# Attention, an MLP and a top-2 mixture of experts in one kernel: ranking queued later, five early groups, first softmax scaled on ScalarE, two 128-row groups last

## The chip, the cores and the metric

The kernel runs on one core of a Trainium2 chip. The metric is the device time of one execution in microseconds (us). The engines are TensorE (PE, with its weight loads as PEld), VectorE (DVE), ScalarE (ACT), GpSimd (POOL) and SyncE (SP, which here issues most transfers). Each takes its instructions in the order in which the program wrote them, so an instruction that waits holds up all behind it on its engine.

## What is computed

Three stages, each feeding the next, for T = 2304 tokens of 512 numbers, all in float32 accuracy:

```python
scores = scale * q @ k.T                       # 4 batches, 8 heads, 576 positions, 64 per head
scores = where(0 <= i - j < 128, scores - slope[h] * abs(i - j), -1e9)
attn = exp(scores - max);  attn /= attn.sum() + 1e-9
x = (attn @ v) as (2304, 512)
x = softplus(x @ w_in) @ w_out                 # 512 -> 2048 -> 512
noisy = x @ w_gate + log1p(exp(x @ w_noise)) * noise      # 8 experts
top2, weights = the two largest of each token, softmax over the two
out[token] += weight * (relu(x[token] @ w1[e]) @ w2[e])   # 512 -> 1024 -> 512, for each choice e
```

## The kernel before

**Tiles.** The MLP works on nine chunks of 256 tokens and on sixteen slices of its 2048 hidden columns. A step t is one slice of one chunk: `mm1` (12 products of 128x256 columns, rows `h<-xh,w` and `h<-xl,w`), a softplus that passes through ACT, DVE and POOL, and three steps later `mm2` (rows `y<-w,gh` and `y<-w,gl`). Numbers are split in a high and a low part (`xh`, `xl`; `gh`, `gl`; `whi`, `wlo`), so one product takes three passes.

**Order of the work.** The first six slices of every chunk run first, and the attention units (20 blocks of up to 128 query rows, four steps m of two heads each) are fed in between, as each chunk's input needs them. Then the last ten slices of chunk 0, of chunk 1 and so on to chunk 8. After each of these a chunk's result is complete, and its routing is fed in by `route(c)`: one entry per half step, where `None` is a half step with nothing. The routing steps are the transposes of the result, the gate's product (`r_logits`), its transposition back (`r_sum`, rows `t<-ident,lgp`) with a chain of some twenty small DVE instructions that finds the two experts (`r_top2`, which ends in the marks `r_mb`), and the ranking `r_rank` (rows `t<-r_mb,tri`): small products that count how many tokens chose each expert so far. The rank is the token's place in its expert's list, and four scatters per chunk write the token and its weight there (`rect<-rec,pi`, issued from POOL; each waits until the one before has landed).

**Groups.** The experts' stage works on groups of one expert: pairs of 128 rows (256 rows, high and low parts) and singles (128 rows, in plain float32). Which expert and which rows a group has is only known at run time. A small table on DVE holds it: `early_table` after the count of chunk 6, for groups that are already full, and `late_table` after chunk 8, for the others. SP reads the table into registers, loads each group's list (`rc<-rect`) and its weights (eight tiles of 512 KB, `raw2` or `rawp`), and POOL gathers the rows (`xg<-x1buf,rc`), 128 at a time. PE transposes them (`t<-ident,xg`). A pair has eight rounds, each an up product (`h<-xh,whi` and the like) and a down product. At the end of a group each 128 rows are scaled (`ys`) and added to the output by a scatter that accumulates (`out<-ys,rc`); such scatters also wait for each other.

**Planner.** The order on each engine is set by the class `Order`: the program is written in PE's order, and it keeps a rough clock with an assumed cost for each instruction. A `chain` is a list of instructions on other engines; each is written out when the clock says that it could run. What is written by the planner runs in that order, whatever the real durations are. In a chain, "A" is ACT, "V" DVE, "P" POOL.

**The lines that the change touches.** In `step_a`, a pair of head blocks gets its scores by PE, DVE adds the bias and finds the maximum, ACT takes the exponential and its sum, DVE the reciprocal (`rec`, lines 357 and 358), and `norm` (line 362) multiplies both blocks by it on POOL; only then can PE transpose them (`step_b`). In `w_convert` the first weights of the MLP (stored as float64) are made from their two integer halves by ACT, DVE and POOL; its last instruction `low` (line 495) runs on DVE or, for each third tile, on POOL. The main loop calls `early_table` at `last_start`, the first step of chunk 8's last ten. The constants `NEARLY` and `nsure` fix how many groups of which kind there are.

Of the kernel before, what the change touches and what calls it, by code (L numbers as in the profile page):

```python
# [99 lines left out]
def cv(n):  # L100
    return 0.15 + n * 0.00104
# [6 lines left out]
def cg(n):  # L108
    return 0.05 + n * 0.00275
# [3 lines left out]
def moe_chain_kernel(ctx, tc, qk, v, w_in, w_out, w_gate, w_noise, noise, w1, w2, out):  # L113
# [18 lines left out]
    NCV = 5  # L132
    NPAIR = (2 * T // P + E - 1) // 2 - 3
    NSING = E - 1
    NEARLY = 3
    NOPT = 2
    NLATE = NPAIR - NEARLY
    TPAD = T + P
# [185 lines left out]
    def step_a(m0):  # L324
# [7 lines left out]
        for x in range(2):  # L332
            hp = (m0 + x) % 4
            for j in range(2):
# [2 lines left out]
                          qkT[hd, sl, 1, hp, :], start=True, stop=True)  # L337
                spend(2.0 * n / 2.4)
        st = tl(att, [P, 4, 4], F32, "st", NST, ("a", m0 + 1))
        for x in range(2):  # L340
            s = tl(att, [P, 512], F32, "s", NS, ("be", m0 + x))
            s = s.rearrange("p (h t) -> p h t", h=2)
            M[m0 + x] = dict(s=s)
            for j in range(2):
                def tail(s=s, x=x, j=j):
                    DVE.tensor_tensor_reduce(s[:nq, j, :n], ps[j][:nq, x, :n],
                                             relh[:nq, 2 * (m0 % 4 + x) + j, r0:r0 + n],
                                             -(D ** -0.5), 3.0e38, OP.add, OP.min, st[:nq, 0, 2 * x + j:2 * x + j + 1])

                def ex(s=s, x=x, j=j):  # L350
                    y = slice(2 * x + j, 2 * x + j + 1)
                    ACT.activation(s[:nq, j, :n], s[:nq, j, :n], AF.Exp, bias=st[:nq, 0, y], scale=-1.0,
                                   accum_out=st[:nq, 1, y])
                chain(("V", cv(n), tail, ("ttr", m0 + x, j)), ("A", ca(n) + 0.2, ex, ("ex", m0 + x, j)))
# [4 lines left out]

        def norm(x):  # L360
            s = M[m0 + x]["s"]
            POOL.tensor_tensor(s[:nq, :, :n], s[:nq, :, :n],  # L362
                               st[:nq, 3, 2 * x:2 * x + 2, None].to_broadcast([nq, 2, n]), OP.mult)
        chain(("V", 0.6, rec, None, [("ex", m0 + x, j) for x in range(2) for j in range(2)]),
              ("P", cg(2 * n), lambda: norm(0), ("a", m0)), ("P", cg(2 * n), lambda: norm(1), ("a", m0 + 1)),
              after=4 * cv(n) + ca(n) + 0.4)

    def step_b(m):
# [98 lines left out]
    def w_convert(i):  # L467
# [24 lines left out]

        def low():
            t = W[i]
            (DVE if LOWV[i % len(LOWV)] else POOL).tensor_tensor(t[:, 1], f32(d["a"]), f32(t[:, 0]), OP.subtract)

        def store():
            if i in sidx:
# [3 lines left out]
              ("A", ca(512), first), ("A", ca(512), third), ("V", 2.2, bits),  # L502
              ("P", cg(512), lambda: POOL.tensor_tensor(d["a"], d["a"], d["raw"][:, :, 0], OP.add), ("wa", i)),
              ("A", ca(512), high),
              ("V", cv(512), low, ("wl", i)) if LOWV[i % len(LOWV)] else ("P", cg(512), low, ("wl", i)),
              (None, 0.0, lambda: mark_now(("w", i), ("wl", i))),
              ("SP", 0.06, store, ("st", i)))

# [259 lines left out]
    def route(c):  # L768
        for _ in range(3):
            yield None  # L770
        yield lambda: r_transpose(c, 0)
        yield lambda: r_transpose(c, 1)
        if c + 1 < NCH:
            yield lambda: part_load(c + 1)
        yield lambda: r_logits(c)
        yield None
        yield lambda: r_sum(c)
        yield None
        yield None
        yield None  # L780
        yield lambda: r_rank(c)
        if c == NCH - 1:
            yield None
            yield lambda: late_table(c)
# [216 lines left out]
    ip = is_ = 0  # L1001
    nsure = NSING - NOPT
    while ip < NLATE or is_ < nsure:
        if ip == NLATE or (is_ + 1 < nsure and is_ * NLATE <= (ip - 2) * nsure):
            groups.append((1, "singles", is_))
            is_ += 1
        else:
            groups.append((2, "pairs", ip))
            ip += 1
# [304 lines left out]
    for t in range(NT + max(L2, len(items) + 2)):  # L1314
# [18 lines left out]
            fed, gap, gaps = 0, 0, 2 * n - 2  # L1333
        if t == last_start:
            open_p2()
            early_table(NCH - 3)
        if t < NT:
            c, fc = jobs[t]
# [91 lines left out]
```

## Time and profile before

| | us |
|---|---|
| median of three runs (1182.83 to 1188.4) | 1184.91 |
| the profiled execution | 1184.44 |
| its span, first to last instruction | 1182.6 |
| PE busy | 1085.8 (92%) |
| DVE busy | 733.9 (62%) |
| ACT busy | 615.2 (52%) |
| POOL busy | 529.3 (45%) |

TensorE's clock is granted at one of two levels, 1.2 and 2.4 GHz. The profile gives it as a share of the full one; the mean is 0.960 here. PE's idle time and the stretches at the lower level are spread unevenly: the page's slices show PE below nine tenths in the first three, in the 22nd, in the 25th and in the last of forty. The shares of a whole run say little about what one stage waits for, so the stages are read apart.

### The profile page before, as it was taken

Reading aid. Unit: us, or ns where it says so; the run is one execution under the profiler, and the core shown is the slowest. Engines: PE = TensorE matmul, PEld = TensorE weight load, DVE = VectorE, ACT = ScalarE, POOL = GpSimd, SP = SyncE. Lnnn points to the kernel's source line nnn. Section 1 sums busy time; section 2 is a strip of 40 time slices with the busy share of each in tenths; the row PEclk is TensorE's granted clock in tenths of the full one; section 3 lists DMA queues with packets and bytes.
Section 4 is the critical chain, followed back from the end, with each engine's and each line's share of the span. In section 5 each row is a group of like instructions: output and inputs, shape, how many; then the busy total and the mean of one; then the engine's idle time right before and its main releaser. Section 6 shows DMA issues by size and latency. Waiting matters only on the chain. (4 is left out here: it accounts for less than half of the span.)

```text
span 1182.6 us, 20591 instructions
## 1 busy us (share of the span) xinstructions
PE 1085.8 (92%) x7021; PEld 924.0 (78%) x7021; DVE 733.9 (62%) x1896; ACT 615.2 (52%) x1443; POOL 529.3 (45%) x547
## 2 busy tenths in 40 slices
PE   4689999999999999999996994999999999999995
PEld 3467777777788888888875894988988988989993
DVE  8985798988875565565567683544544545635640
ACT  5676787877754444444434451544544545535531
POOL 3765677866665555556555131123223222223211
PEclk8689999999999999999997997999999999999998
DMA  7231443555673211212209429779789788788722
GB/s 293 98 90 54 174 167 129 206 196 179 215 271 117 74 70 55 72 46 64 72 23 391 121 53 352 215 211 292 213 241 263 210 248 262 207 259 251 190 36 28
DMA packets 79276, 198.31 MB, mean 168 GB/s; under 512 B 17153, under 2 KB 27521, under 8 KB 79169
## 3 DMA queue, kind: packets, MB, share of 16 engines
q1 hardware_dynamic: 68832, 175.43, 44.2%
q0 software_dynamic: 10336, 21.54, 9.3%
q8 instruction: 56, 0.92, 0.3%
q14 instruction: 52, 0.42, 0.1%
HBM read 157.70 MB, written 39.25 MB: 167 GB/s over the span
## 5 line engine op out<-in xcount | busy, mean ns | idle before, releaser
L190 PE MATMUL h<-xh,w 128*128 128x256 f32 x1152 | 243.7, 294 | 5.0 <-ACT xh L420 2.6
L1235 POOL DMA_INDIRECT out<-ys,rc x41 | 82.4, 2010 | 350.4 <-DVE ys L1244 207.9
L190 PEld LDWEIGHTS h<-xh,w 128*128 128x128 f32 x1152 | 194.3, 196 | 18.5 <-DVE sl L559 6.4
L1121 DVE TENSOR_TENSOR wlo<-rawp,whi 128x1024 fp32r<-128x1024 f32 x106 | 129.5, 1222 | 117.5 <-ACT whi L1123 117.3
L190 PE MATMUL y<-w,gh 128*128 128x512 f32 x552 | 182.8, 413 | 1.0 <-DVE x L633 1.0
L190 PE MATMUL h<-xl,w 128*128 128x256 f32 x576 | 166.4, 289 | 4.1 <-DVE xl L425 4.1
L1123 ACT ACTIVATE whi<-rawp 128x1024 fp32r<-128x1024 f32 x106 | 112.3, 1059 | 110.0 <-PE h L190 102.5
L190 PE MATMUL h<-xh,whi 128*128 128x256 f32 x576 | 165.8, 288 | 0.0
L565 POOL TENSOR_TENSOR su<-sa,su 128x256 f32<-128x256 f32 x144 | 111.0, 771 | 119.4 <-DVE su L564 83.8
L190 PE MATMUL h<-xh,wlo 128*128 128x256 f32 x576 | 163.0, 283 | 0.0
L190 PE MATMUL h<-xl,whi 128*128 128x256 f32 x576 | 163.0, 283 | 0.0
L556 ACT ACTIVATE sa<-h 128x256 f32<-128x256 f32 x144 | 54.9, 381 | 169.0 <-PE h L190 133.6
L560 POOL TENSOR_TENSOR sl<-sl,su 128x256 f32<-128x256 f32 x144 | 110.8, 770 | 22.0 <-DVE sl L559 13.4
L190 PEld LDWEIGHTS h<-xl,w 128*128 128x128 f32 x576 | 113.1, 196 | 7.2 <-DVE xl L425 4.5
L190 PEld LDWEIGHTS h<-xh,whi 128*128 128x128 f32 x576 | 110.0, 191 | 7.8 <-DVE gl L1174 1.0
L190 PEld LDWEIGHTS h<-xl,whi 128*128 128x128 f32 x576 | 110.0, 191 | 7.4 <-issue 1.9
L190 PEld LDWEIGHTS y<-w,gh 128*128 128x128 f32 x552 | 97.6, 196 | 18.7 <-issue 3.2
L190 PE MATMUL y<-w,gl 128*128 128x512 f32 x276 | 110.0, 399 | 0.0
L190 PEld LDWEIGHTS h<-xh,wlo 128*128 128x128 f32 x576 | 109.9, 191 | 0.0
L362 POOL TENSOR_TENSOR s<-s,st 128x512 f32<-128x512 f32 (+2 forms) x80 | 81.0, 1021 | 34.3 <-DVE st L358 21.5
L1173 ACT ACTIVATE gh<-h 128x256 fp32r<-128x256 f32 x144 | 54.1, 376 | 63.3 <-PE h L190 60.5
L564 DVE TENSOR_SCALAR su<-sa 128x256 f32<-128x256 f32 x144 | 60.3, 419 | 41.8 <-ACT sa L557 41.0
(255 smaller groups left out, 2285.5 us busy)
## 6 DMA issues: line engine op xcount, KB each, us to landing
rawp<-in_moe_w SPq DMA_DIRECT2D x137, 512.0 KB, 5.0
raw<-in_moe_w SPq DMA_DIRECT2D x47, 512.0 KB, 4.5
qkT<-in_qk SPq DMA_DIRECT2D x20, 512.0 KB, 5.1
raw<-in_moe_w_in SPq DMA_DIRECT2D x16, 512.0 KB, 5.2
raw<-in_moe_w_out SPq DMA_DIRECT2D x16, 512.0 KB, 6.4
out<-zero SPq DMA_DIRECT2D x19, 256.0 KB, 5.6
xspill<-xh SPq DMA_DIRECT2D x9, 512.0 KB, 2.6
xspill<-xl SPq DMA_DIRECT2D x9, 512.0 KB, 4.0
```

The lines of the kernel that those rows point to most:

```text
L190: PE.matmul(o, l, r, start=start, stop=stop)
L362: POOL.tensor_tensor(s[:nq, :, :n], s[:nq, :, :n], st[:nq, 3, 2 * x:2 * x + 2, None].to_broadcast([nq, 2, n]), OP.mult)
L556: chain(("A", ca(CT), lambda: ACT.activation(a, ph, AF.Abs)), ("A", ca(CT), lambda: ACT.activation(a, a, AF.Exp, scale=-1.0), ("e", t)), ( ...
L560: ("P", cg(CT), lambda: POOL.tensor_add(l, l, u), None, (("d", t),)),
L564: chain(("V", cv2(CT), lambda: DVE.tensor_scalar(u, a, 1.0, 1.0, op0=OP.add, op1=OP.subtract), None, (("e", t),)), ("P", cg(CT), lambda: P ...
L565: ("P", cg(CT), lambda: POOL.tensor_tensor(u, a, u, OP.subtract), ("d", t)), after=2 * ca(CT) + 0.15)
L1121: DVE.tensor_sub(lo, t, f32(hi))
L1123: chain(("A", ca(1024), lambda: ACT.activation(hi, t, AF.Copy), None, (("r2", j),)), ("V", cv(1024), low, ("w2", j)))
L1173: chain(("A", ca(CT), lambda: ACT.activation(gh, ph, AF.Relu)), ("V", cv(CT), lambda: DVE.scalar_tensor_tensor(gl, ph, 0.0, f32(gh), op0=O ...
L1235: POOL.indirect_dma_start(out=out[:, :], out_offset=bass.IndirectOffsetOnAxis(ap=rc[:, a, 0:1], axis=0), in_=ys, in_offset=None, compute_o ...
```

## The change

- `NEARLY` goes from 3 to 5: five groups of 256 rows come from the early table and 13 instead of 15 from the late one. The early table is made three steps later.
- In `route`, `r_sum` comes half a step later and `r_rank` comes seven half steps behind it instead of four.
- For attention units 0 to 3 (the inputs of the first two chunks), the scaling by the reciprocal goes from POOL (one instruction for two blocks) to ACT (one for each block, 32 in all).
- For the first 12 weight tiles, `low` is always on DVE; four of them were on POOL.
- With E for an early pair, P for a late pair and S for a single, the order of groups was EEEPPSPPPSPPPSPPPSPPPPS, and it is now EEEEEPPSPPPSPPPSPPPPPSS.

```diff
-    NEARLY = 3
+    NEARLY = 5
...
+        first = u <= attn_last(1)
...
         def norm(x):
             s = M[m0 + x]["s"]
+            if first:
+                for j in range(2):
+                    ACT.activation(s[:nq, j, :n], s[:nq, j, :n], AF.Copy, scale=st[:nq, 3, 2 * x + j:2 * x + j + 1])
+                return
             POOL.tensor_tensor(s[:nq, :, :n], s[:nq, :, :n],
                                st[:nq, 3, 2 * x:2 * x + 2, None].to_broadcast([nq, 2, n]), OP.mult)
         chain(("V", 0.6, rec, None, [("ex", m0 + x, j) for x in range(2) for j in range(2)]),
-              ("P", cg(2 * n), lambda: norm(0), ("a", m0)), ("P", cg(2 * n), lambda: norm(1), ("a", m0 + 1)),
+              *[("A", 2 * ca(n), lambda x=x: norm(x), ("a", m0 + x)) if first else
+                ("P", cg(2 * n), lambda x=x: norm(x), ("a", m0 + x)) for x in range(2)],
               after=4 * cv(n) + ca(n) + 0.4)
...
-            (DVE if LOWV[i % len(LOWV)] else POOL).tensor_tensor(t[:, 1], f32(d["a"]), f32(t[:, 0]), OP.subtract)
+            (DVE if (i < 2 * NA or LOWV[i % len(LOWV)]) else POOL).tensor_tensor(t[:, 1], f32(d["a"]), f32(t[:, 0]), OP.subtract)
...
-              ("V", cv(512), low, ("wl", i)) if LOWV[i % len(LOWV)] else ("P", cg(512), low, ("wl", i)),
+              ("V", cv(512), low, ("wl", i)) if (i < 2 * NA or LOWV[i % len(LOWV)]) else ("P", cg(512), low, ("wl", i)),
...
         yield lambda: r_logits(c)
         yield None
+        yield None
         yield lambda: r_sum(c)
-        yield None
-        yield None
-        yield None
+        for _ in range(6):
+            yield None
         yield lambda: r_rank(c)
...
-        if ip == NLATE or (is_ + 1 < nsure and is_ * NLATE <= (ip - 2) * nsure):
+        if ip == NLATE or (is_ + 2 < nsure and is_ * NLATE <= (ip - 2) * nsure):
...
         if t == last_start:
             open_p2()
+        if t == last_start + 3:
             early_table(NCH - 3)
```

On ACT, in the first 20 to 30 us, this stood between the exponentials (L352, tile `s` with its sums in `st`) of attention unit 1, first two of its head pairs and last two (weights' steps: L477 and L481 read `raw`, L491 writes the high part `w`):

```order
L352 ACTIVATE s,st<-s,st 128x256 x2
L477 ACTIVATE cva<-raw 128x512
L481 ACTIVATE raw<-raw 128x512
L352 ACTIVATE s,st<-s,st 128x256
L491 ACTIVATE w<-cva 128x512
L352 ACTIVATE s,st<-s,st 128x256
L420 ACTIVATE xh<-t 128x2x128
L388 ACTIVATE pT<-y 128x512
```

Now the same exponentials (L353) are followed by the scalings of that unit (L365, `s<-s,st`), between the weights' steps:

```order
L353 ACTIVATE s,st<-s,st 128x256 x3
L497 ACTIVATE w<-cva 128x512
L353 ACTIVATE s,st<-s,st 128x256
L487 ACTIVATE raw<-raw 128x512
L365 ACTIVATE s<-s,st 128x256 x2
L497 ACTIVATE w<-cva 128x512
L483 ACTIVATE cva<-raw 128x512
L487 ACTIVATE raw<-raw 128x512
L365 ACTIVATE s<-s,st 128x256 x4
L497 ACTIVATE w<-cva 128x512
```

The scalings joined ACT's row; POOL has none of them left for these units, and its row there holds only the weights' additions.

On PE, at the end of the MLP, this stood around the ranking of chunk 7: it came between the two transposes (`xg`) of the first group, before the MLP's last up product (`h<-xh,w`):

```order
L201 MATMUL t<-ident,xg 128x128 x4
L190 MATMUL y<-w,gh 128x512 x2
L190 MATMUL y<-w,gl 128x512
L190 MATMUL y<-w,gh 128x512 x2
L190 MATMUL y<-w,gl 128x512
L190 LDWEIGHTS tri
L190 MATMUL t<-r_mb,tri 128x8
```

Now the ranking of chunk 7 comes behind the first up product of the experts' stage (its last rows are the first three below):

```order
L190 MATMUL h<-xh,whi 128x256
L190 MATMUL h<-xl,whi 128x256
L190 MATMUL h<-xh,wlo 128x256
L190 MATMUL y<-w,gh 128x512 x2
L190 MATMUL y<-w,gl 128x512
L190 MATMUL y<-w,gh 128x512 x2
L190 MATMUL y<-w,gl 128x512
L190 LDWEIGHTS tri
L190 MATMUL t<-r_mb,tri 128x8
```

The ranking moved behind both transposes and one round; both transposes now stand ahead of it, with nothing but the MLP's products between them.

On POOL, at the same place, this followed chunk 6's four scatters (`su` and `sl` are the softplus of the steps still open; L762 the scatters of the lists, L1030 the gathers, L1235 the scatters to the output):

```order
L1030 DMA xg<-x1buf,rc 128x512 x2
L565 TENSOR_TENSOR su<-sa,su 128x256
L560 TENSOR_TENSOR sl<-sl,su 128x256
L565 TENSOR_TENSOR su<-sa,su 128x256
L560 TENSOR_TENSOR sl<-sl,su 128x256
L565 TENSOR_TENSOR su<-sa,su 128x256
L1030 DMA xg<-x1buf,rc 128x512 x2
```

Now (L768 scatters of the lists, L1036 gathers, L1241 scatters to the output, L571 and L566 the softplus):

```order
L1036 DMA xg<-x1buf,rc 128x512 x4
L571 TENSOR_TENSOR su<-sa,su 128x256 x2
L566 TENSOR_TENSOR sl<-sl,su 128x256 x2
L571 TENSOR_TENSOR su<-sa,su 128x256
L566 TENSOR_TENSOR sl<-sl,su 128x256
L768 DMA rect<-rec,pi 18688x2 x4
L1036 DMA xg<-x1buf,rc 128x512 x2
L1241 DMA out<-ys,rc 2432x512 x2
L768 DMA rect<-rec,pi 18688x2 x4
L1036 DMA xg<-x1buf,rc 128x512 x2
```

The gathers of the first two groups now stand together, ahead of three steps' softplus; those of the third and of the fourth group each stand behind four scatters, of chunk 7 and of chunk 8.

## Rows read from the trace of the kernel before

**Rows 1.** PE's waits over the span: who waited for whom, us, times, longest.
```profile
PE t L190 <- DVE r_mb L695: 20.3, 9, 4.6
PE t L201 <- DMA xg<-x1buf,rc: 15.5, 1, 15.5
PE y L201 <- POOL s L362: 14.4, 4, 7.2
PE t L201 <- POOL s L362: 5.0, 5, 2.3
```
**Rows 2.** Stretches of 20 us: PE, PEld, DVE, ACT, POOL busy; granted clock, DMA.
```profile
20.00:40.00 20.00, 10.98 (x56) 7.38 (x56) 19.62 (x40) 9.55 (x28) 12.76 (x11) 0.59 0.26 103
40.00:60.00 20.00, 12.88 (x76) 9.28 (x76) 19.39 (x41) 15.86 (x39) 14.64 (x12) 0.75 0.40 144
480.00:500.00 20.00, 17.91 (x109) 15.05 (x108) 11.54 (x52) 7.70 (x22) 8.44 (x11) 0.91 0.21 76
620.00:640.00 20.00, 11.72 (x57) 9.74 (x55) 16.14 (x33) 10.60 (x22) 13.26 (x14) 0.83 0.99 387
```
**Rows 3.** Timeline of the start: start, duration (us), engine, instruction, [idle before].
```profile
14.72 0.43 DVE L486 TENSOR_SCALAR cva<-cva 128x512 int32<-128x512 int32 x1
20.58 2.22 POOL L362 TENSOR_TENSOR s<-s,st 128x512 f32<-128x512 f32 x2 [0.39 <-DVE st L358]
20.66 1.24 DVE L485 TENSOR_SCALAR cva<-cva 128x512 f32<-128x512 f32 x1
21.94 1.15 DVE L486 TENSOR_SCALAR cva<-cva 128x512 int32<-128x512 int32 x1
62.43 1.41 DVE L487 SCALAR_TENSOR_TENSOR cva<-raw,cva 128x512 int32<-128x512 int32 x1
```
**Rows 4.** ACT's groups by shape: two of the first 80 us, then one line's groups.
```profile
L420 ACT ACTIVATE xh<-t 128x256 fp32r<-128x256 f32 x8 | 2.9, 368 | 1.5 <-PE t L190 1.5
L388 ACT ACTIVATE pT<-t 128x512 f32<-128x512 f32 x4 | 2.4, 588 | 3.0 <-PE t L201 3.0
L1241 ACT ACTIVATE ys<-z,rc x12: 668/671/687, 682.2 to 1169.9; 128x512 f32<-128x512 f32 x12
```
**Rows 5.** Timeline of PE in the routing of chunk 3: transposition back, and ranking.
```profile
484.91 0.33 PE L201 MATMUL t<-ident,lgp 96*128 96x96 f32 x2
492.99 0.18 PE L190 MATMUL t<-r_mb,tri 128*128 128x8 bf16 x1 [2.09 <-DVE r_mb L695]
```
**Rows 6.** Timelines around the experts' start (PE, POOL, SP's queue); last, line 762's landings.
```profile
596.34 0.18 PE L190 MATMUL t<-r_mb,tri 128*128 128x8 bf16 x1 [2.09 <-DVE r_mb L695]
611.50 0.98 POOL L762 DMA_INDIRECT rect<-rec,pi  x1 [1.98 <-DVE c_Eoff L862]
615.16 3.00 SPq L1021 DMA_DIRECT2D rc<-rect  x3
619.59 0.99 POOL L1030 DMA_INDIRECT xg<-x1buf,rc  x1 [4.85 <-issue]
647.53 0.27 PE L190 MATMUL h<-xh,whi 128*128 128x256 f32 x1
...
DMA to landing us min/median/max: 2.1/3.0/5.7
```
**Rows 7.** Line 1030, gathers: ns min/median/max, landings; PE's timeline behind the long wait; clock.
```profile
L1030 POOL DMA_INDIRECT xg<-x1buf,rc x41: 942/1008/2041, 619.6 to 1123.6; - x41
DMA to landing us min/median/max: 3.4/6.5/8.9
...
725.58 1.09 PE L201 MATMUL t<-ident,xg 128*128 128x128 f32 x4 [15.47 <-DMA xg<-x1buf,rc]
729.00:731.00 2.00, 2.00 (x15) 0.93 1.01 397
```
**Rows 8.** Timeline of the end: ACT, POOL.
```profile
1169.89 0.69 ACT L1241 ACTIVATE ys<-z,rc 128x512 f32<-128x512 f32 x1 [6.27 <-PE z L190]
1170.12 1.56 POOL L1235 DMA_INDIRECT out<-ys,rc  x1 [4.95 <-issue]
1175.76 1.55 POOL L1235 DMA_INDIRECT out<-ys,rc  x1 [4.08 <-issue]
```

## The prediction, made before the changed kernel had run

> **What bounds the kernel now.** The list of PE's waits comes first [rows 1]: four lines hold 55 us of waiting, and each belongs to one place. Then the stretches of 20 us show what the other engines and the clock did there [rows 2]; the timelines give the durations.
>
> *The start.* PE waits 14.4 + 5.0 = 19.4 us for the scaling by the reciprocal on POOL [rows 1]. Between 20 and 60 us DVE is busy 19.62 and 19.39 of 20 us [rows 2], so the late scaling is mostly DVE's doing: the reciprocal stands in its queue. And DVE is slowed by POOL: the integer step of the weights takes 0.43 us, but 1.15 us while two scalings run on POOL [rows 3].
>
> *The MLP's second half, 340 to 620 us.* PE waits nine times for `r_mb`, 20.3 us together, the longest 4.6 [rows 1]. In the routing of chunk 3 the transposition back is at 484.91 us and the ranking at 492.99, of which 2.09 us are the wait [rows 5]. Two steps lie between, so a step is (492.99 - 2.09 - 484.91) / 2 = 3.0 us, and the marks come 8.1 us after the transposition. No other engine is above 58% in that stretch [rows 2]: the ranking is simply asked for too early. Three such stretches show a granted clock of 0.91 (one of the three that read alike is in [rows 2]); PE was idle for 2.09 us just before its rows there became twice as long.
>
> *The head of the experts' stage.* From 620 to 640 us PE works 11.72 of 20 us, at a clock of 0.83, and the stretch behind it reads 0.83 too [rows 2].
>
> *The fourth group.* One wait of 15.5 us for a gather [rows 7].
>
> *The end.* The last 128 rows are scaled by 1169.89 + 0.69 = 1170.58 us, but their scatter is issued at 1175.76, behind that of the rows before at 1170.12 [rows 8].
>
> **The change part by part.**
>
> *Scaling on ACT, `low` on DVE.* Sixteen POOL instructions leave, four for each of units 0 to 3, of up to 1.11 us each (two in 2.22 us, [rows 3]); 32 on ACT come. The trace has none like these. A copy of 128x512 takes 588 ns and one with a scale from a column 671, so the column adds 83 ns; a copy of 128x256 takes 368 [rows 4]. That makes 451 ns at most for each, 32 x 0.451 = 14.4 us of ACT, whose idle time in the two stretches of rows 2 alone is 40 - 25.4 = 14.6 us. What leaves POOL no longer delays DVE: in the timeline nine DVE instructions between 20.66 and 62.43 us overlap a scaling (the first two and the last are in [rows 3]), and their excess over the same form alone sums to 5.6 us by my count. The four `low` that come to DVE cost it about 0.7 us each; three of its instructions lose a similar delay, so I put this at nothing. Since DVE is the stage's limit I take 5.6 us. The bounds are 0 (ACT's full row brings the scalings as late as POOL did) and 19.4 (all of that waiting).
>
> *Ranking later.* Between transposition and ranking there are now seven half steps, 3.5 x 3.0 = 10.5 us, against 8.1 needed. Without the longest, which is chunk 7's and belongs to the next part, the waits sum to 20.3 - 4.6 = 15.7 us (chunks 0 to 6 and 8). The stretches at 0.91 give back 3 x 20 x 0.09 = 5.4 us. DVE, ACT and POOL have room, and PE has no other wait to fall into here. Bounds 0 and 21.1; I take 21.1, since 2.4 us remain in hand.
>
> *Early table three steps later.* Here a new wait comes. The chain from the ranking of chunk 6 is: marks to last scatter 611.50 - 596.34 = 15.2 us, list load at +18.8, gather at +23.3 (619.59), and its landing 6.5 later, at +29.7 [rows 6, 7]. The weights `rec` will lie ready before the later ranking, which may shorten the scatters' start by up to 2 us: 28 us. PE, in its new order, has seven steps and one up product between that ranking and the first transposition of gathered rows, 7.5 x 3.0 = 22.5 us. So PE waits about 5.5 us for the gather, followed by about 3.4 us lost to the low clock (half of the two stretches' 2 x 20 x 0.17 = 6.8). It replaces 20 - 11.72 = 8.3 us of idle time and the 6.8: the causes of these, weights that DVE and ACT convert in the middle of chunk 7's routing, come later by as much. Gain 15.1 - 8.9 = 6.2 us. The weights come behind five list loads instead of three, at 1.0 us each [rows 6]: 2.0 us later, which I take off in full. What is queued behind the four gathers on POOL is the softplus of three open steps; PE needs these only after the transpositions, so they cost nothing unless the gathers take longer. Bounds: 0 and 15.1.
>
> The median gather takes POOL 1.008 us and the longest of 41 took 2.041 [rows 7]. The Trainium skill, SBUF — State Buffer, in "SBUF: two separate sides", says that a transfer issued from GpSimd stands still while VectorE runs a two-port instruction, since its descriptors can't be written; its example goes from 620 to about 3100 ns. By that page the first landing would be some 2.5 us later and the sum that much smaller, an estimate; by the rows the longest would cost 1.0 us. The trace has the direction, not the size.
>
> *Five early groups.* The fourth group no longer needs the late table; the sixth does. Two groups of eight rounds lie between. Twenty rounds were done from 647.53 [rows 6] to the start of the wait, 725.58 - 15.47 = 710.11 [rows 7], 3.1 us each, so it is 16 x 3.1 = 50 us of work, against a wait of 15.5 us and a ranking that is two steps (6 us) later. 28 us remain in hand. Gone is the wait of 15.5 us and the time at the low level behind it: PE's rows are twice as long from 725.58 to about 729 us, and from 729 to 731 the clock reads 0.93 [rows 7], 1.7 us. Together 17.2; the bounds are 10 (the wait partly comes back elsewhere) and 17.2.
>
> *Two singles last.* With a pair ahead of the last single, two scatters of the pair and one of the single queue up; with a single ahead it is one and one, so the last is issued when its rows are ready, 1175.76 - 1170.58 - 0.2 = 5.0 us sooner. PE does the same products. Bounds 0 and 5.2.
>
> **Sum.** 5.6 + 21.1 + 6.2 - 2.0 + 17.2 + 5.0 = 53.1 us. The profiled execution took 1184.44 us (0.47 below the median of the three), so 1131.3 us.
>
> **The rivals.**
>
> *The gathers and weights of the first group come later than I work out (1142 us).* The transfers are near their limit there, 0.99 of the engines' time at 387 GB/s [rows 2]. If the first gather takes the longest times seen, 2.04 instead of 1.01 and 8.9 instead of 6.5 us [rows 7], PE's wait grows by 3.4, and if the weights land behind four gathers by another 7. For it: four gathers now stand together. (The rule of the Trainium skill that is named above speaks for it too.) Against it: the weights are asked for after them, so the first gather meets less traffic than before.
>
> *ACT's row brings no gain (1137 us).* ACT was busy 15.86 of 20 us from 40 to 60 [rows 2]; in the new order three of a unit's four scalings stand behind weights' steps.
>
> *The ranking waits all the same (1152 us).* The small DVE instructions are written by the planner's clock, so they could move back with the ranking. Against it: they start with the transposition, which moves by half a step only.
>
> *Slower than before: the lists of the third and fourth group.* Their gathers stand on POOL behind four scatters of chunk 7 and of chunk 8, each of which waits for the landing of the one before, 3.0 us in the median and 5.7 at most [rows 6]. At 5.7 the third group's list is late by some 6 us and the fourth's too. To be slower than before, 8 scatters would have to lose 59 us, from about 13 us for each landing on. No row is near that.
>
> **How the numbers follow.** My forecast has 0.62, the late first group 0.16, no gain at the start 0.10, the ranking 0.07, the lists 0.05 (of which 0.03 go beyond the bound). The predicted time is 1131 us. Its own range, with the start between 0 and 10, the head between 0 and 12 and the end between 2 and 5, is 1119 to 1144. The range for 8 in 10 takes in all but the worst of the rivals: 1116 (every bound on the good side, but the start at 10) to 1150. A change of 0.5%, 6 us, is about what a measurement of this kernel can tell from none. All cases but the last end more than 0.5% faster: 0.95 faster, 0.02 within, 0.03 slower.
>
> **What would show it.** In the profile after: no wait for `r_mb` above 0.5 us; no wait of PE for a gather behind 700 us; one for the first gather of 3 to 8 us just ahead of the experts' stage; PE's waits for the scaled `s` (then from ACT) under 10 us; the last scatter within 1 us of its rows. It is wrong if the wait of the fourth group only moves to the sixth, if ACT's row makes PE wait as long as POOL's did, or if weights are waited for in the first group.

## The result and the profile after

The changed kernel takes 1144.39 us (median of 4 runs, 1144.15 to 1147.89), the kernel before 1183.87 beside it; the ratio is 0.9668 (0.9634 to 0.9702). It is faster by 39.5 us where 53.1 were forecast. The profiled execution is the longest of the four (1147.89, span 1146.1), so its spans show some 3 us less of the gain than the medians do.

PE's waits after, in the form of [rows 1] (some lines left out):

```profile
PE y L201 <- ACT s L365: 15.1, 3, 6.7
PE t L201 <- DMA xg<-x1buf,rc: 10.1, 3, 6.2
PE t L201 <- ACT s L365: 7.1, 1, 7.1
PE h L190 <- ACT xh L1054: 6.8, 1, 6.8
...
PE t L201 <- POOL s L367: 4.0, 4, 2.4
...
PE h L190 <- DVE xl L1055: 2.3, 1, 2.3
PE t L190 <- DVE mcum L754: 2.0, 1, 2.0
```

The 20.3 us for `r_mb` are gone, and so is the single wait of 15.5. In chunk 8 the ranking now waits 2.0 us for its running count `mcum`. But PE still waits for the scaling: 22.2 us for ACT and 4.0 for POOL, which scales the later units, where it was 19.4 in all before. New waits have come into the first groups of the experts' stage. Two of the stretches of [rows 2], and three of the experts' stage:

```profile
20.00:40.00 20.00, 9.62 (x62) 6.56 (x64) 19.55 (x47) 19.95 (x54) 7.57 (x6) 0.69 0.23 90
480.00:500.00 20.00, 20.00 (x135) 17.96 (x134) 15.89 (x57) 9.11 (x23) 11.92 (x15) 1.00 0.23 80
618.33:638.33 20.00, 17.66 (x105) 15.77 (x106) 12.47 (x35) 6.24 (x13) 3.43 (x4) 0.84 1.03 404
660.00:680.00 20.00, 18.03 (x119) 16.26 (x118) 15.70 (x48) 9.30 (x14) 5.46 (x4) 1.00 0.80 186
680.00:700.00 20.00, 13.81 (x78) 12.29 (x77) 10.01 (x27) 7.55 (x11) 9.70 (x7) 0.83 0.67 132
```

The third of them begins with the first up product of the experts' stage. The same 20 us before:

```profile
647.53:667.53 20.00, 20.00 (x134) 17.64 (x133) 9.35 (x15) 8.44 (x15) 6.59 (x7) 1.00 0.77 222
```

In the MLP PE is full and at the full clock. ACT has no idle time left from 20 to 40 us, and DVE has as little as before.

To place the gain, the span is cut at the same instructions of both traces. PE's timeline before gives two of them, the first transposition of chunk 0 and of chunk 7 for routing:

```profile
376.53 0.60 PE L201 MATMUL t<-ident,x 128*128 128x128 f32 x4
613.10 0.60 PE L201 MATMUL t<-ident,x 128*128 128x128 f32 x4
```

The same two after, then the turning (transposition) of the first group's rows, the first up product and the turning of the fourth group:

```profile
374.91 0.60 PE L201 MATMUL t<-ident,x 128*128 128x128 f32 x4
589.94 0.60 PE L201 MATMUL t<-ident,x 128*128 128x128 f32 x4
606.25 0.63 PE L201 MATMUL t<-ident,xg 128*128 128x128 f32 x4 [2.60 <-DMA xg<-x1buf,rc]
618.33 0.58 PE L190 MATMUL h<-xh,whi 128*128 128x256 f32 x1 [6.83 <-ACT xh L1054]
692.26 1.09 PE L201 MATMUL t<-ident,xg 128*128 128x128 f32 x4 [6.19 <-DMA xg<-x1buf,rc]
```

| stretch | before, us | after, us | gain | forecast |
|---|---|---|---|---|
| start, to chunk 0's transposition | 376.5 | 374.9 | 1.6 | 5.6 |
| to chunk 7's transposition (ranking) | 236.6 | 215.0 | 21.5 | 21.1 |
| to the first up product (head) [rows 6] | 34.4 | 28.4 | 6.0 | 4.2 |
| to the last scaling `ys` (five groups) [rows 8] | 522.4 | 520.2 | 2.1 | 17.2 |
| to the end of the span (last groups) | 12.7 | 7.5 | 5.2 | 5.0 |

The sum is 36.4, the spans differ by 36.5. So the shortfall has two places: the start, and the part where five early groups were to bring 17.2.

ACT's timeline at the head shows the waiting for the first up product (L1129 converts weights, one more of them starts at 611.64; L1054 converts the gathered rows, their second half at 617.69); its last row is the last scaling of the end:

```profile
609.96 1.06 ACT L1129 ACTIVATE whi<-raw 128x1024 fp32r<-128x1024 f32 x1 [5.83 <-DMA raw<-in_moe_w]
...
613.92 1.06 ACT L1129 ACTIVATE whi<-raw 128x1024 fp32r<-128x1024 f32 x1 [0.93 <-DMA raw<-in_moe_w]
614.88 0.58 ACT L1054 ACTIVATE xh<-t 128x512 fp32r<-128x512 f32 x1
...
1138.57 0.69 ACT L1247 ACTIVATE ys<-z,rc 128x512 f32<-128x512 f32 x1 [6.13 <-PE z L190]
```

PE had the gathered rows at 606.25, after a wait of only 2.6 us. Their conversion stands behind three conversions of weights, which wait for weights to land. SP's queue shows when these were asked for, behind five lists:

```profile
598.87 5.10 SPq L1027 DMA_DIRECT2D rc<-rect  x5
605.45 1.86 SPq L1100 DMA_DIRECT2D raw<-in_moe_w  x4
```

POOL's timeline, chunk 8's scatters with the fourth group's gather, and the last scatter to the output:

```profile
668.35 0.99 POOL L768 DMA_INDIRECT rect<-rec,pi  x1 [0.30 <-DVE c_Lbig L868]
674.26 0.97 POOL L768 DMA_INDIRECT rect<-rec,pi  x1 [4.92 <-DVE c_LAofoh L868]
678.93 0.95 POOL L768 DMA_INDIRECT rect<-rec,pi  x1 [3.70 <-DMA rect<-rec,pi]
684.11 1.59 POOL L768 DMA_INDIRECT rect<-rec,pi  x1 [4.22 <-DMA rect<-rec,pi]
686.00 0.98 POOL L1036 DMA_INDIRECT xg<-x1buf,rc  x1 [0.31 <-PE h L190]
...
1139.53 1.56 POOL L1241 DMA_INDIRECT out<-ys,rc  x1 [5.75 <-ACT ys L1247]
```

The gather is issued as soon as the fourth scatter is through, 17.65 us after the first. The last scatter is issued 0.27 us after its rows are scaled (1138.57 + 0.69), no longer behind another scatter.

### The profile page after: what moved, and what is told of

Same layout as the page of the kernel before. It is cut to its first block, busy times and chain, and to the rows that moved or that the text cites. A ratio compares the mean times of both kernels' runs of the same rounds, so it can differ in the third digit from the quotient of the medians.

```text
span 1146.1 us, 20654 instructions
## 1 busy us (share of the span) xinstructions
PE 1072.6 (94%) x7021; PEld 915.6 (80%) x7021; DVE 730.2 (64%) x1900; ACT 622.6 (54%) x1475; POOL 501.2 (44%) x527
## 4 chain that ended last, share of the span: by engine, by line
PE 80%; DVE 11%; ACT 3%; DMA 2%; issue 2%; POOL 1%; POOLq 0%; SPq 0%; ACTq 0%; DVEq 0%
PE h L190 36%; PE y L190 23%; PE z L190 11%; PE t L201 4%; PE t L190 3%; PE t L336 2%; DVE s L347 2%; DVE gl L569 1%; DMA xg<-x1buf,rc 1%; ACT s L353 1%; DVE cva L492 1%; DVE cva L493 1%; DVE cva L491 1%; DVE su L570 1%; DVE w L501 1%
## 5 line engine op out<-in xcount | busy, mean ns | idle before, releaser
L190 PE MATMUL h<-xh,w 128*128 128x256 f32 x1152 | 240.0, 291 | 1.0 <-DVE sl L565 0.9
L1241 POOL DMA_INDIRECT out<-ys,rc x41 | 81.5, 1987 | 341.7 <-DVE ys L1250 179.1
L190 PEld LDWEIGHTS h<-xh,w 128*128 128x128 f32 x1152 | 191.8, 194 | 14.6 <-DVE sl L565 4.8
L1129 ACT ACTIVATE whi<-rawp 128x1024 fp32r<-128x1024 f32 x106 | 112.4, 1061 | 127.5 <-PE h L190 114.3
L190 PE MATMUL y<-w,gh 128*128 128x512 f32 x552 | 178.7, 405 | 0.0
L571 POOL TENSOR_TENSOR su<-sa,su 128x256 f32<-128x256 f32 x144 | 112.0, 777 | 106.5 <-DVE su L570 85.8
L190 PEld LDWEIGHTS h<-xh,whi 128*128 128x128 f32 x576 | 110.7, 192 | 14.6 <-ACT xh L1054 7.3
L566 POOL TENSOR_TENSOR sl<-sl,su 128x256 f32<-128x256 f32 x144 | 111.2, 773 | 20.2 <-DVE sl L565 5.6
L190 PEld LDWEIGHTS y<-w,gh 128*128 128x128 f32 x552 | 94.8, 191 | 16.5 <-issue 2.9
L353 ACT ACTIVATE s<-s,st 128x256 f32<-128x256 f32 (+2 forms) x160 | 76.1, 478 | 18.1 <-DVE st L347 17.8
L569 DVE TENSOR_TENSOR gl<-sl,gh 128x256 fp32r<-128x256 f32 x144 | 76.4, 531 | 9.0 <-ACT gh L567 6.4
```

Of the source, the lines that this page charges most:

```text
L190: PE.matmul(o, l, r, start=start, stop=stop)
L566: ("P", cg(CT), lambda: POOL.tensor_add(l, l, u), None, (("d", t),)),
L569: ("V", cv(CT), lambda: DVE.tensor_sub(gl, l, f32(gh)), ("g", t)))
L571: ("P", cg(CT), lambda: POOL.tensor_tensor(u, a, u, OP.subtract), ("d", t)), after=2 * ca(CT) + 0.15)
L1129: chain(("A", ca(1024), lambda: ACT.activation(hi, t, AF.Copy), None, (("r2", j),)), ("V", cv(1024), low, ("w2", j)))
L1241: POOL.indirect_dma_start(out=out[:, :], out_offset=bass.IndirectOffsetOnAxis(ap=rc[:, a, 0:1], axis=0), in_=ys, in_offset=None, compute_o ...
```

## The experiments

The first four kernels take one part each out of the changed kernel. They ran beside the kernel before at 1186.38 us, the next four at 1184.79, the three after them at 1184.91, the last at 1183.77. So the ratio to the kernel before is given for each, and medians are compared directly only within one of these sets; 0.001 of the ratio is 1.2 us. The base is f_base below, the changed kernel with nothing edited.

**u_start.** No scaling on ACT, `low` on POOL for every third weight.

```diff
-        first = u <= attn_last(1)
+        first = False
...
-            (DVE if (i < 2 * NA or LOWV[i % len(LOWV)]) else POOL).tensor_tensor(
+            (DVE if LOWV[i % len(LOWV)] else POOL).tensor_tensor(
...
```

> The changed kernel with its first part undone: all scalings on POOL and the subtraction of the weights' low half on POOL for every third weight again. By the prediction's term for the start the time rises by 5.6 us, to 1150.0. By the profile of the changed kernel, where the first chunk's transposition comes only 1.6 us earlier than before and PE waits 22.2 us for the scaling on ACT instead of 19.4 for that on POOL, it rises by 1.6 us, to 1146.0. If ACT's full row costs more than POOL's it falls, to 1143 or less. The first part's place in the profile is the transposition of chunk 0 for routing: 376.5 us in this kernel by the second theory, 380.5 by the first.

Measured: 1145.28, ratio 0.9654 (0.9631 to 0.9678): not slower than the changed kernel. Chunk 0's transposition comes at 377.2 us. In the trace the first part of the change is worth 2.3 us there against the profile after (4.4 against that of f_base); in the time nothing shows. The time is no clean test of the start, though: the wait for the fourth group's gather is 2.0 us here, where it is 6.2 after and 4.8 in f_base, so a later start is in part taken up there.

**u_rank.** The ranking two steps earlier, alone.

```diff
+        yield lambda: r_sum(c)
         yield None
-        yield lambda: r_sum(c)
-        for _ in range(6):
-            yield None
+        yield None
+        yield None
         yield lambda: r_rank(c)
```

> The changed kernel with the old place of the ranking alone (two steps earlier); the early table stays where it is. By the prediction's term the time rises by 21.1 us, to 1165.5: PE waits for r_mb 15 to 16 us in all in chunks 0 to 6 and 8, and three stretches of 20 us show a granted clock near 0.91. A rival: the clock's share is no cost of these waits, then 15.7 us and 1160. Another: the small DVE instructions move with the ranking, so that no wait comes back, 1144. The wait for the first gather and what stands behind it stays as in the changed kernel.

Measured: 1163.91, ratio 0.9811 (0.9785 to 0.9837), so 0.0142 of 1184.8, 17 us, above the base. PE's waits from 300 to 600 us, and from 380 to 1140:

```profile
PE t L190 <- DVE r_mb L701: 15.6, 7, 3.0
...
PE t L190 <- DVE r_mb L701: 30.6, 9, 12.9
PE t L201 <- DMA xg<-x1buf,rc: 0.8, 1, 0.8
```

Chunks 0 to 6 wait 15.6 us again (14.1 in the kernel before, which is 20.3 less the 4.6 of chunk 7 and the 1.6 of chunk 8), and four stretches between 460 and 600 us read a clock of 0.91 or 0.92 again. From chunk 0's transposition to chunk 7's it takes 238.4 us (375.33 to 613.70), 23.3 more than after: the ranking's term is confirmed. Chunk 7 now waits 12.9; the waits for `xh` and for the fourth gather are gone instead, so part of it is given back and only 17 us show in the time. That what stands behind the first gather stays as it was did not hold.

**u_three.** Three early groups.

```diff
-    NEARLY = 5
+    NEARLY = 3
```

> The changed kernel with three groups from the early table, the rest as it is. The fourth group then needs the late table, whose ranking is now 6 us later than in the kernel before: PE waits 15.5 + 6 = 21.5 us for its gather and loses 1.7 us to the clock, 23.2 us. By the prediction nothing of this is given back by five groups, so the time rises by 23 us, to 1167. By the profile of the changed kernel the wait of 6.2 us for the fourth group's gather, the later one of 1.3 and 2.3 us at the low clock belong to five groups: they go, and the rise is 13 us, to 1157. A rival: late table and late gather no longer bind, since the groups ahead take longer; then the rise is under 5 us.

Measured: 1143.83, ratio 0.9638 (0.9613 to 0.9664): no loss at all. The 1167 and 1157 expected were wrong; the rise of under 5 us that the rival named came true, but not for its reason, since the late gather still makes PE wait. PE's waits between 590 and 720 us, POOL's scatters of chunk 8, and the stretch from 660 to 680 us:

```profile
PE t L201 <- DMA xg<-x1buf,rc: 19.3, 2, 13.3
```
```profile
659.51 1.04 POOL L768 DMA_INDIRECT rect<-rec,pi  x1 [0.30 <-issue]
663.69 0.97 POOL L768 DMA_INDIRECT rect<-rec,pi  x1 [3.15 <-DVE c_LAp L868]
666.11 0.96 POOL L768 DMA_INDIRECT rect<-rec,pi  x1 [1.45 <-DMA rect<-rec,pi]
669.01 0.95 POOL L768 DMA_INDIRECT rect<-rec,pi  x1 [1.94 <-DMA rect<-rec,pi]
```
```profile
660.00:680.00 20.00, 19.06 (x126) 17.27 (x124) 17.00 (x51) 9.86 (x16) 5.03 (x5) 1.00 0.18 25
```

The fourth group waits 13.3 us for the late table, and is turned at 692.40 us, where five early groups turn it at 692.26. The other wait is of 6.0 us, for the first gather. With three, SP loads two lists fewer ahead of the weights (the first weight is asked for 3.6 us behind the first list, 598.58 to 602.17, instead of 6.6, 598.87 to 605.45) and PE does not wait for `xh`; and there are no weights of a fourth group to load while the ranking of chunk 8 is written, so DMA is busy 0.18 instead of 0.80, and the scatters stand 2.4 to 4.2 us apart instead of 4.7 to 5.9. Five early groups had bought the early list at the price of all of this; that the loads are what slows the scatters is read from the comparison and was not tested by itself.

**u_single.** One single last.

```diff
-        if ip == NLATE or (is_ + 2 < nsure and
+        if ip == NLATE or (is_ + 1 < nsure and
```

> The changed kernel with one group of 128 rows at the end instead of two. By the prediction the time rises by 5.0 us, to 1149.4, with the last scatter issued about 5 us behind the scaling of its rows. A rival: what the profile shows at the end (7.6 us from PE's last product to the end of the span instead of 12.7) comes from the landing of the scatters and not from the order of the groups; then the time stays within 1 us of 1144.4.

Measured: 1149.54, ratio 0.9684 (0.9659 to 0.9709), 1.8 us above the base by the ratios (4.1 by medians, which are of two sets); the time alone does not settle it. The trace does, in ACT's and POOL's timeline of the end:

```profile
1135.75 0.69 ACT L1247 ACTIVATE ys<-z,rc 128x512 f32<-128x512 f32 x1 [6.27 <-PE z L190]
...
1141.29 1.55 POOL L1241 DMA_INDIRECT out<-ys,rc  x1 [3.82 <-issue]
```

The rows are ready at 1136.44, their scatter is 4.85 us late; after the change it is 0.27 us behind its rows. From the last scaling to the end of the span it takes some 12 us (to 1147.8) instead of 7.5, so the order of the groups makes the difference, and not the landing of the scatters.

**f_base.** The changed kernel, nothing edited.

> The changed kernel once more, unchanged, as the base for the kernels beside it: ratio 0.967 to the kernel before, and the same waits of PE: 6.8 us for the converted first input, 6.2 us for the fourth group's gather.

Measured: 1145.44, ratio 0.9669 (0.9650 to 0.9689). Its span is 1142.6; PE waits 6.8 us for `xh`, 2.3 for `xl` and 4.8 for the fourth group's gather, and chunk 0's transposition comes at 372.8. The start thus differs by 2 us between two executions of one kernel, and by this profile it gained 3.8 us, not 1.6.

**f_head.** At most one conversion of weights ahead of the first group's input.

```diff
-        if j >= wl[0] or nsplit[0] >= NSPLIT or ...
+        if j >= wl[0] or nsplit[0] >= (NSPLIT if 0 in turned else 1) or ...
...
                     turned.add(0)
+                    pump()
```

(`pump` lets the conversions go on as soon as the first group is turned.)

> The changed kernel, in which only one conversion of the experts' weights may be written ahead of the first group's input (in the changed kernel three of them stand ahead of the first half on ACT and two more ahead of the second). The theory: the wait of 6.8 us before the first up product comes from these conversions, which wait for weights to land, and not from the gather. Then the input is converted by about 612.5, the first up product starts at 613 instead of 618.3, the wait of 2.3 us for xl goes too and part of the 3.5 us that PE loses to the clock: 6 to 9 us less than the base. The rival: the weights of the second and third rounds are late in any case; then the wait moves to wlo and the gain is 0 to 2 us. By the prediction's step, in which the gather is what PE waits for here, nothing changes.

Measured: 1146.06, ratio 0.9665 (0.9645 to 0.9686): nothing. PE's waits behind 380 us, and ACT's timeline:

```profile
PE t L201 <- DMA xg<-x1buf,rc: 9.7, 4, 6.5
PE h L190 <- ACT xh L1054: 2.9, 1, 2.9
PE h L190 <- DVE xl L1055: 2.6, 1, 2.6
...
PE h L190 <- DVE gl L1180: 1.9, 1, 1.9
```
```profile
609.24 1.06 ACT L1129 ACTIVATE whi<-raw 128x1024 fp32r<-128x1024 f32 x1 [6.34 <-DMA raw<-in_moe_w]
```

The order of the conversions was not the cause of the lost time, though the trace had named it. It did set the first up product, which now comes 240.0 us behind chunk 0's transposition (613.70 less 373.70) instead of 242.9 in f_base, but PE reaches the ranking of chunk 8 no sooner (282.9 against 282.2 us behind the same point). The one conversion that is left still waits until 609.24 for its weight; what waited for `xh` now waits for `xh`, `xl` and `gl`. The late thing is the weights, as the next kernel shows.

**f_lists.** The lists of groups 2 to 4 behind the first four weights (the second piece is in the loader of the experts' weights, behind each load).

```diff
-        for g in range(NEARLY):
+        for g in range(2):
             g_rows(g)
...
+        if wl[0] == 4:
+            for g2 in range(2, NEARLY):
+                g_rows(g2)
```

> The changed kernel with the lists of groups 2 to 4 loaded behind the first four loads of weights instead of ahead of them. Three list loads take 1.02 us each on SP (five in 5.10 us), so the first weights are asked for 3.1 us earlier. If the weights set the start of the first up product, it comes 3 us earlier and the time falls by 3 to 4 us. The prediction counted 1.0 us for each load, so it agrees in size. The rival: the weights land when the transfers allow it, 0 to 1 us.

Measured: 1139.51, ratio 0.9606 (0.9585 to 0.9628), 5.9 us below the base (7.5 by the ratios), more than either theory gave. SP's queue, PE's waits for gathers behind 380 us, and the turning of the first group:

```profile
598.47 1.61 SPq L1027 DMA_DIRECT2D rc<-rect  x2
600.89 1.94 SPq L1100 DMA_DIRECT2D raw<-in_moe_w  x4
```
```profile
PE t L201 <- DMA xg<-x1buf,rc: 11.2, 2, 6.1
```
```profile
609.54 1.09 PE L201 MATMUL t<-ident,xg 128*128 128x128 f32 x4 [6.12 <-DMA xg<-x1buf,rc]
```

The first weight is asked for 2.4 us behind the first list, in the changed kernel 6.6 us: three lists cost 4.2 us, 1.4 each with the reading of the table in between, and not 1.0. Both conversions' waits are gone (9.1 us), and a wait of 6.1 for the first gather stands there instead of 2.0. The gather itself came later: PE goes on 7.6 us after its issue begins (601.96 to 609.54), in the changed kernel 3.6 us after it (602.66 to 606.25). All kernels here divide by this. In the seven with five lists ahead of the weights, the first weight is asked for 1.3 to 2.8 us after the first gather's issue begins, and PE goes on 3.5 to 3.7 us after it. In the six with two or three lists (u_three, this one and those below but f_gather), the weight is asked for 0.2 to 1.4 us ahead of the gather, and PE goes on 6.7 to 7.6 us after it. So lists ahead of the weights made the weights late, but kept the gather clear of them; that it is their traffic which slows the gather is read from this division and not tested by itself.

**f_gather.** Gathers a group earlier.

```diff
-            if g < 2 or g - 1 in turned:
+            if g < 2 or g - 2 in turned:
                 g_start(g)
...
-                    if g + 2 in REG:
-                        g_start(g + 2)
+                    if g + 3 in REG:
+                        g_start(g + 3)
```

> The changed kernel with each gather from the third group on asked for a group earlier, so that the fourth group's stands ahead of the four scatters of chunk 8 on POOL and the third group's ahead of those of chunk 7. The theory: five early groups gained nothing so far because the fourth group's gather stands behind scatters that land 5 us apart; then the wait of 6.2 us for it goes, with the 2.3 us at the low clock behind it: 8.5 us less than the base. A rival: the gather lands late because the transfers are full and not because of its place; then no change. Another: the third group's gather now stands ahead of POOL's softplus of the last two steps and waits for its buffers, which costs PE 2 to 3 us at the head, a gain of 5 to 6 us only.

Measured: 1136.12, ratio 0.9597 (0.9576 to 0.9618), 9.3 us below the base (8.5 by the ratios). The one of PE's waits behind 380 us that is for gathers:

```profile
PE t L201 <- DMA xg<-x1buf,rc: 2.0, 1, 2.0
```

Only the first gather is waited for; the waits for `xh` and `xl` are as they were. The scatters of chunk 8 are as slow as before (664.48, 670.34, 675.20, 679.74), but the fourth group's gather went out at 645.68. So it was the gather's place that cost the time, and not the slowness of the scatters alone.

**f_comb, f_comb_split, f_gather3.** Both edits together; both, with half of the start's scalings on POOL again (`if first and x == 0` at both places); the earlier gathers alone with `NEARLY = 3`.

> The changed kernel with both edits that shortened it: gathers asked for a group earlier, and the lists of groups 2 to 4 behind the first weights. The two act on different waits (the fourth group's gather near 690 us; the head near 610 us), so the theory expects their sum, 8.5 + 6 = 14 us less than the base, about 1131, ratio 0.955. The rival: both are the same shortage of transfers, and what one frees the other takes; then about 9 us, 1136.

> The kernel of both edits, and at the start one of a pair's two scalings on POOL again, the other on ACT. The changed kernel fills ACT there (19.95 of 20 us busy from 20 to 40 us) and the one before had PE wait for POOL; if the start is bound by whichever engine does all of the scaling, the stage ends 2 to 4 us sooner. If DVE sets it (19.55 of 20 us busy there), POOL's return slows DVE again and nothing is gained: within 1 us, or up to 2 us longer.

> The kernel with earlier gathers, but with three groups from the early table. If five early groups are worth nothing by themselves but are worth their price once the fourth gather stands ahead of chunk 8's scatters, this one waits for the late table as the three-group kernel did (13 us, fourth group turned at 692 us): about 1144, 8 us above the kernel with earlier gathers and five groups. The rival: earlier gathers help for another reason; then it is within 3 us of 1136.

Measured: f_comb 1131.21, ratio 0.9546 (0.9524 to 0.9569); f_comb_split 1130.84, 0.9554 (0.9530 to 0.9578); f_gather3 1143.97, 0.9657 (0.9631 to 0.9683). The two edits nearly add up (14.6 us below the base by the ratios, where they bring 7.5 and 8.5 alone), and f_comb beats both kernels; behind 380 us PE waits only these times in it, and its first up product and last scaling are these:

```profile
PE t L201 <- DMA xg<-x1buf,rc: 5.7, 1, 5.7
PE t L190 <- DVE mcum L754: 2.0, 1, 2.0
```
```profile
615.80 0.28 PE L190 MATMUL h<-xh,whi 128*128 128x256 f32 x1
...
1121.93 0.69 ACT L1250 ACTIVATE ys<-z,rc 128x512 f32<-128x512 f32 x1 [6.13 <-PE z L190]
```

Cut like the table above (chunk 0's transposition at 373.58, chunk 7's at 588.61, the end of the span at 1129.6), the gains are 2.9, 21.5, 7.2, 16.2 and 5.0 us. Once gather and lists have their places, the five early groups bring nearly the 17.2 us that were forecast for them.

Three early groups cost 7.1 us by the ratios once gathers are early (0.9657 against 0.9597), and nothing without: five early groups and the place of the gathers only pay together. The split of the scaling brings nothing, though ACT is no longer full; from 20 to 40 us:

```profile
20.00:40.00 20.00, 11.30 (x56) 7.31 (x56) 19.59 (x43) 13.53 (x37) 9.47 (x8) 0.53 0.22 88
```

**f_dve.** On top of f_comb, one DVE instruction less in each of the first 12 weights.

```diff
-            DVE.tensor_scalar(f32(a), f32(a), F64_LO, F64_HI, op0=OP.max, op1=OP.min)
+            if i >= 2 * NA:
+                DVE.tensor_scalar(f32(a), f32(a), F64_LO, F64_HI, op0=OP.max, op1=OP.min)
```

> The kernel of both edits, without one DVE instruction in each of the first twelve weights (the clamp of values outside single precision's range is left out there): twelve of 0.57 us, 6.8 us of DVE in the start; nothing moves on any engine. If DVE is what bounds the start, whoever scales, the transposition of chunk 0 comes 4 to 7 us sooner (from about 374 us) and the time falls as much, to about 1125.5. If ACT's row is the bound, or the order of the row, nothing is gained: within 1.5 us of 1131.2.

Measured: 1130.76, ratio 0.9553 (0.9532 to 0.9573), chunk 0's transposition at 372.5: nothing. From 40 to 60 us DVE falls to 16.85:

```profile
40.00:60.00 20.00, 12.04 (x92) 9.54 (x90) 16.85 (x43) 17.04 (x45) 7.77 (x7) 0.76 0.39 144
```

In f_comb it is 19.55 there. From 20 to 40 us, however, DVE stays full in f_dve too (19.72). So taking work from DVE alone, or from ACT alone, does not shorten the start; no kernel here took work from both.

## Why the prediction was right, and where it was not

The time, 1144.4 us, lies in the range that was given 8 chances in 10 (1116 to 1150) and just past the end of the forecast's own range (1119 to 1144). It lies there because the ranking and the end came as worked out; of the other 27.0 us only 9.7 came in the trace. The rival of 1142 us is near in time but not in its cause: the first gather came sooner than worked out, not later.

**Start: wrong in its premise.** The step "since DVE is the stage's limit I take 5.6 us" fails. DVE lost 5.1 us of work up to 120 us in f_dve and ACT 6.7 in f_comb_split (against f_comb), and neither shortened the kernel. Chunk 0's transposition came at 376.5 and 377.2 us in the two profiles with all scalings on POOL and at 371.1 to 375.6 in the twelve others (median 373.6): some 3 us, hardly more than executions of one kernel differ, but on the same side in all twelve. A queue that is busy 19.6 of 20 us is full, but its fullness was no proof that work taken from it shortens the stage. The prediction's rival (ACT's row brings no gain) is nearer to what happened: PE waits 22.2 us for ACT and 4.0 for POOL, where it waited 19.4 for POOL. The price of a scaling was low too: the 32 take 497 ns in the median and 509 at most, where 451 was called the most. What sets the start's length stays open: the order in which instructions stand on the engines is the candidate that no run here varied by itself.

**Ranking: right, and in its parts.** 21.5 us in the trace against 21.1. Moving only the ranking back brought back 15.6 us of waiting in chunks 0 to 6, where 14.1 had been, and the clock near 0.91. The loss of that run is smaller (17 us), since the head then waits less. One part was missed: chunk 8's 1.6 us for `r_mb` did not go, but became 2.0 for `mcum`.

**Early table and lists: the size was near by luck, the cause was not.** The forecast was a wait of 5.5 us for the first gather, and 2.0 us for two more lists ahead of the weights. It was 2.6 us for the gather, since this took 3.6 us and not the 6.5 of the sum, and 6.8 and 2.3 for weights: the two lists cost 3.0 us (6.6 against 3.6 in u_three), not 2.0, and this was the path that ended last. The stage began 6.0 us sooner, but the 20 us behind the first up product, full and at the full clock before, lose 20 - 17.66 x 0.84 = 5.2 us to the wait for `xl` and to the clock, so 0.8 remain of 4.2. f_lists shows both sides: with the weights early, the gather takes 7.6 us and the wait for it is 6.1.

The Trainium skill, SBUF — State Buffer, in "SBUF: two separate sides", would have transfers issued from GpSimd held up while VectorE runs a two-port instruction. The trace bears out the direction: of the 41 gathers after, the median issue took 1.004 us and the longest 2.050, as before [rows 7], and the four longest (1.74 to 2.05) each began 0.05 to 0.34 us after a subtraction `wlo` of 1.2 us on DVE had begun. The four of the head met none and took 0.95 to 1.04, so this cost the head nothing; no run here shows the page's 3100 ns.

**Five early groups: the step that failed most.** The forecast counted 17.2 us as gone; 2.1 came. "28 us remain in hand" was about the sixth group and held: no wait stands there. The error was to count the fourth group as done once its list came from the early table. Its gather is also an instruction on POOL, behind four scatters that each wait for the one before to land. The prediction had this as its last rival, and gave the landings 3.0 us, 5.7 at most [rows 6], a delay of some 6 us and a chance of 0.05. It came: 4.7 to 5.9 us apart, a wait of 6.2 us, and a stretch at 0.83 behind it. The table's 2.1 us are the 17.2 less the 5.2 behind the first up product, 6.2 + 2.3 at the fourth group and 1.3 for a later gather, which leaves 2.2. The five groups themselves contributed to this, since the early list lets the weights of the next groups load while the scatters land. That those loads slow the scatters is argued from kernels that differ so (u_three and f_gather3 against those with five early groups); that the gather's place was the cause of the wait is shown by f_gather, and that the 17.2 were there to be had by f_comb, with 16.2.

**End: right.** 5.2 us in the trace against 5.0; the last scatter is issued 0.27 us behind its rows.

Of the rows that were to show it: no wait for `r_mb`, the last scatter beside its rows and almost no gather behind 700 us (one of about 1.3 us) came true; waits for the scaled `s` under 10 us did not, and the first gather's came 0.4 us short. Of its three signs of being wrong two came: ACT's row makes PE wait as long as POOL's did, and weights are waited for in the first group. The third, a wait that moves on to the sixth group, did not.

## What to carry to other kernels

A wait that is removed uncovers the next one at the same place: for each late thing ask what else the same instruction needs, on every queue, and where its own issue stands in line. Moving a decision earlier (here which rows a group has) pays only when everything between the decision and its use, the list load, the gather's issue and the weights, moves too. The instruction that the trace names as the last releaser may only be first in the row: here moving it away brought nothing, and loading earlier what it waited for brought 5.9 us.

## What the runs showed of the hardware

- Chained scatters of 128 rows of 8 bytes each stood 2.4 to 4.2 us apart with DMA busy 0.18 of the time (u_three), and 4.7 to 5.9 us apart at 0.80 (the changed kernel).
- The first gather let PE go on 3.5 to 3.7 us after its issue began where the first 512 KB weight was asked for after it, and 6.7 to 7.6 us where the weight was asked for ahead of it (seven and six kernels).
- In the profile after, the four gathers that POOL began to issue 0.05 to 0.34 us behind the start of a `wlo` on DVE took 1.74 to 2.05 us to issue instead of 1.0; one that began 0.04 us behind one took 1.00.
- The 20 us behind the first up product read 0.84 of the clock and those around the fourth gather's wait 0.83: 17.66 x 0.16 = 2.8 and 13.81 x 0.17 = 2.3 us on top of the waits themselves.
- Two executions of the same kernel reached the first transposition of chunk 0 at 374.9 and 372.8 us; differences of 2 us in the start can't be read from single profiles.
